# Fourier mixing: mirrored rows in another order, and the third piece of the second stage made once for two batches

## Chip, cores and metric

The kernel runs on one core of one Trainium2 chip. The metric is the device time of one execution in microseconds: 1210.03 us before, the median of three runs (1209.47 to 1211.12). The core has TensorE (PE, with its weight loads as PEld), VectorE (DVE), ScalarE (ACT), GpSimd (POOL) and SyncE (SP), which here only issues DMAs.

## The reference

Eight batches of eight heads, 576 positions, head size 64. Attention is causal by blocks of 64; its output x has 512 columns per position. Then comes a two-dimensional Fourier transform whose real part is added to x, a normalization, and a feed-forward layer (a feed, below).

```python
attn = softmax(where(mask, q @ k.T / 8, -1e9)); x = heads side by side of (attn @ v)   # 8 x 576 x 512
X = np.fft.fft(np.fft.fft(x, axis=1), axis=2)
u = x + np.real(X)
un = (u - mean(u)) / sqrt(var(u) + 1e-6)
out = u + np.maximum(un @ w_ch1, 0.0) @ w_ch2        # 512 -> 2048 -> 512
```

## The kernel before, in words

Every product is made in halves, a high and a low part of each operand, so that three products (high by high, high by low, low by high) stand for one. The inner loops all run on 128-row tiles; nearly every vector instruction is recorded under line 211 and every product under line 244, since two helpers issue them, so the names of tiles tell what they are.

**Attention.** Each of the 64 heads h gives five steps: a row maximum (`max_part`, `pair_max`), its transposition as a shift (`shift`, a DMA lead<-mt), the scores and their exponentials (`scores`: PSUM tile, ACT exp to p and cast to ph, POOL subtraction to pl), the value products (`values`, 45 products into av) and a division (DVE: DEN, rec, x). The x of two heads is written by DMA to a DRAM tile xd of the batch.

**Fourier, one batch b (`fourier_steps`, L862).** A real transform over 576 positions needs only the sums and differences of row s and its mirror 576 - s, so `mirror` (L865) loads rows in order (X, tiles LL) and mirrored rows by an indirect DMA (U, tiles UU), in three pieces c: 128 + 128 + 33 rows. `folded` (L886) makes the sums (name "c") and differences (name "s") of both rows and both column halves, and splits them into high and low part (tiles fs, un). `stage1` (L928) transforms over the positions, into z (zc0, zc1, zs0, zs1), with a middle column apart (`stage1_tail`, ZT). The second stage transforms over the columns: for each piece c, `stage2_sin` (L964) makes six products with z sine as weights, and `stage2_cos` (L980) seven with z cosine and ZT as weights and 258 columns moving; DVE makes difference and sum (dif, add) and POOL adds these to X and U in place (four additions). Piece 2 has 33 weight columns: row 288, which is its own mirror, and 32 pairs. It runs first, then pieces 0 and 1 (the loop at L1035). Row 288's result goes by DMA to row 0 of U piece 0 (L1006), whose mirror would be row 0 itself. The 32 + 32 results of piece 2 go by DMA to half of a tile `left`, which holds those of two batches.

**Feeds.** `normalized_steps` (L1052) normalizes two tiles, transposes them (ident,un) and queues a feed (`feed_steps`, L1112): 192 first products into ps or h (uh, ul), then gh on ACT and gl on DVE, then 96 second products into acc, an addition into u and the store. A batch has a feed for its low rows (X pieces 0 and 1) and one for its up rows (U pieces 0 and 1); four batches share one for the rests (two tiles `left`). That makes 18 feeds. In a batch with b % 4 == 3 the rests come first, then low, then up. Feeds 15 to 17 (`SEVEN`, L55) use a form with seven half products.

**What sets the order.** A planner (the loop at L1557) simulates all steps with assumed costs and emits instructions in its own order; each engine then runs its list strictly in that order. Steps stand in lanes (heads, maxima, scores, values, Fourier); the lanes' first steps compete by their `place`, and the products of the feed at the head of the queue are used as a filler wherever no other step is ready (L1592 to L1616). Feed 1 cannot begin before batch 0 is transformed, after head 7, and needs the weights W, which the side lanes prepare on DVE and ACT. `feed_number` (L1098) tells which feed a later step must wait for: the tiles of batch b - 2 must be free for `mirror`, and one step waits for the feed of the rests.

Of the kernel before, what the change touches and what calls it, by code (L numbers as in the profile page):

```python
# [91 lines left out]
def _constants():  # L92


    n = np.arange(NCOS)
    s = np.arange(LNH + 1)
# [4 lines left out]
    s_s[0] = 0.0  # L101
    s_s[LNH] = 0.0
    s_s[:, 0] = 0.0
    c_s[LNH, :LNH + 1] = (-1.0) ** n[:LNH + 1]
    k = np.arange(KCOL)
# [39 lines left out]
    p = np.arange(P)  # L145
    rows = np.stack([S - p, S - P - p, 320 - p % 32], 1)
    rows[0, 0] = rows[32, 2] = S
    return {
# [69 lines left out]
def tile_attn_fourier_ffn(  # L218
# [86 lines left out]
    for i in range(2):  # L305
        gpsimd.memset(MAIN[i], LEAST)
        gpsimd.memset(MAIN[i][0:64, 0:1], 0.0)
        gpsimd.memset(DIAG[i], LEAST)
    for i in range(HF):
        gpsimd.dma_start(LEAD[i][D:KS], c_masks)  # L310
        vector.tensor_scalar(LEAD[i][0:D, 0:64], ones[0:D, 0:64], 0.0, None, op0=ALU.mult)
    for i in range(2):
        vector.memset(VH[i][:, 0:4, :, D:D + 1], 1.0)
        vector.memset(VH[i][0:64, 4, :, D:D + 1], 0.0)
        vector.memset(VH[i][64:128, 4, :, D:D + 1], 1.0)
    for at in range(0, NCOS, P):
        w = min(P, NCOS - at)
        vector.tensor_scalar(ZT[:, at:at + w], ones[:, 0:w], 0.0, None, op0=ALU.mult)
# [543 lines left out]
    def fourier_steps(b):  # L862
        U, X, low, up, mine = [], [], [], [], []

        def mirror():  # L865
            xd = xs.pop(b)
            LL, UU = utile(), utile()
            U.extend((UU[:, 0], UU[:, 1], work.tile([97, DM], F32, name="U2", bufs=1)))
            X.extend((LL[:, 0], LL[:, 1], work.tile([33, DM], F32, name="X2", bufs=1)))
# [5 lines left out]
            U2 = U[2]  # L875
            sync.dma_start(X[2], xd[256:289])
            sync.dma_start(LL, xd[0:256].rearrange("(c p) d -> p c d", p=P))
            for dst, i in ((U2[0:33], 2), (U[0], 0), (U[1], 1)):
# [7 lines left out]
        def folded(op, width, name, c):  # L886
            r = (128, 128, 33)[c]
            e = work.tile([P, DM], F32, name="tmp", bufs=2)
            vector.tensor_tensor(e[0:r], X[c][0:r], U[c][0:r], op=op)
            vector.tensor_tensor(e[0:r, 1:256], e[0:r, 1:256], e[0:r, 511:256:-1], op=op)  # L890
            yield
# [8 lines left out]
            else:  # L900
# [3 lines left out]
                if name == "c":  # L904
                    rr = [U[2][64 + 32 * a:65 + 32 * a, 0:width].bitcast(F32R) for a in range(2)]
                    scalar.copy(rr[0], e[32:33, 0:width])
                yield
                vector.tensor_tensor(
                    t[32:64, 0:width], e[0:32, 0:width], t[0:32, 0:width].bitcast(F32), op=ALU.subtract
                )  # L910
# [17 lines left out]
        def stage1(name, m):  # L928
# [14 lines left out]
            vector.tensor_tensor(zz[:, 1], t[:, 0:n], zz[:, 0].bitcast(F32), op=ALU.subtract)  # L943
            yield

        def stage1_tail():
# [15 lines left out]
        bss = {}  # L962

        def stage2_sin(c):  # L964
            n = 128 if c < 2 else 32
            t = ps_tile()
            i = 0
            ns = slice(P * c, P * c + n)
            for m in range(2):
                for a, w in ((0, 0), (0, 1), (1, 0)):  # L970
                    mm(t[0:n, 0:KCOL], z["s", m][:, a, ns], sd[:, m, w], start=(i == 0), stop=(i == 5))
                    i += 1
            yield
            bs = bss[c] = work.tile([P, KCOL], F32, name="bs", bufs=1)
            if c == 2:
                gpsimd.memset(bs[32:33], 0.0)
            scalar.copy(bs[0:n], t[0:n, 0:KCOL])
            yield

        def stage2_cos(c):  # L980
            na, nb = (128, 128) if c < 2 else (33, 32)
            t = ps_tile()
            i = 0
            ns = slice(P * c, P * c + na)
            for m in range(2):
                for a, w in ((0, 0), (0, 1), (1, 0)):
                    mm(t[0:na, 0:KCOL], z["c", m][:, a, ns], cd[:, m, w], start=(i == 0), stop=False)
                    i += 1
            mm(t[0:na, 0:KCOL], ZT[:, ns], tail, start=False, stop=True)
            yield  # L990
# [6 lines left out]
            engine = gpsimd  # L997
            for u, lo, hi, n in ((X[c], dif, add, na), (U[c], add, dif, nb)):
                engine.tensor_tensor(u[0:n, 0:257], u[0:n, 0:257], lo[0:n, 0:257], op=ALU.add)
                engine.tensor_tensor(u[0:n, 257:512], u[0:n, 257:512], hi[0:n, 255:0:-1], op=ALU.add)  # L1000
            if c == 2:
                at = 64 * (b % 2)
# [19 lines left out]
        def stages(name):  # L1022
            for m in range(2):
                yield Step(
                    lambda m=m: stage1(name, m), 0.87, ("A0.42", "D0.47"), (D_("f" + name),),
                    D_("z" + name) if m == 1 else None, True, place=place,
                )
            if name == "c":
                yield Step(stage1_tail, 0.62, ("A0.4", "D0.46"), (D_("fc"),), D_("zt"), True, place=place)

        cos, sin = ("c", ALU.add, 257), ("s", ALU.subtract, 256)
        order = (folds(*cos), folds(*sin), stages("c"), stages("s"))
        for steps in order:
            yield from steps
        for c in (2, 0, 1):  # L1035
            yield Step(lambda: stage2_sin(c), 0.67, ("A0.38",), (D_("zs"),), D_("b", c), True, place=place)
            yield Step(
                lambda: stage2_cos(c), 0.78, ("D0.86", "B", "G3.0"), (D_("zc"), D_("zt"), D_("b", c)) + ((("F", feed_number(b - 1, 2)),) if c == 2 and b == 4 else ()), D_("u", c), True,
                place=place,
            )  # L1040
# [595 lines left out]
def _rows():  # L1636

    p = np.arange(P)
    up = S - p
    up[0] = LNH  # L1640
    return np.concatenate([p, P + p, up, S - P - p, 256 + p[0:32], 320 - p[0:32]])

# [23 lines left out]
```

## Time and profile before

| | |
|---|---|
| median of three runs | 1210.03 us (1209.47 to 1211.12) |
| the profiled execution, its own time | 1206.97 us |
| its span, first to last instruction | 1205.2 us |
| mean granted TensorE clock | 0.987 |
| TensorE's first product, end of its last | 8.03 us, 1201.1 us |
| feed 1 begins, heads 7 and 8 end | after 150 us; 95 and 154 us |
| products of the feed's halves | 3456 first, of 10338 in all recorded |

The profile has one row for a group of instructions: the engine, the operation, tile written <- tiles read, shapes and the count. In a timeline the first two columns are the start and the duration in us; a product's duration includes the way through the array, so products that follow each other overlap, and what one costs is read from start to start. "idle before <- X" is the time in which the engine had nothing to do, and what ended it. In the windows each engine's busy time has its count of instructions behind it.

### The profile page before, as it was taken

The page shows a single profiled execution, that of the slowest core. Times are in us where ns is not written, and L with a number is a line of the kernel's source. Part 1 is how long each engine was busy: PE and PEld are TensorE (multiplying, and loading weights), DVE is VectorE, ACT ScalarE, POOL GpSimd, SP SyncE. Part 2 cuts the span into 40 slices and gives each one's busy share as a digit, 9 for nine tenths or more (in the row PEclk, how much of TensorE's full clock was granted, in tenths as well). Part 3 has the DMA queues.
Part 4 walks back from the last instruction along what each step waited for, and adds up shares of the span by engine and source line. Part 5 has one row for each costly group of instructions (what it writes and reads, how often), then busy time and mean ns, then how long its engine had stood idle before and what let it go on. Part 6 is the DMA issues. An engine that isn't in the chain of part 4 may idle for free.

```text
span 1205.2 us, 26322 instructions
## 1 busy us (share of the span) xinstructions
PE 1136.7 (94%) x10338; PEld 839.3 (70%) x10338; DVE 746.8 (62%) x1615; ACT 622.4 (52%) x1338; POOL 487.8 (40%) x639
## 2 busy tenths in 40 slices
PE   5777797999999999999999999999999999999998
PEld 4554475676677777777777777777676767788885
DVE  6887888566867577675666758474657424534421
ACT  5666667755765566556565647654223212233320
POOL 4552625544652455345243355433333310535410
PEclk9998899999799999999999999999999999999999
DMA  8775454333452335242344033231010010000000
GB/s 261 234 231 176 144 132 105 89 111 102 112 136 72 93 84 159 72 119 76 105 116 137 28 100 114 85 95 41 28 41 18 23 58 1 23 10 10 18 18 18
DMA packets 66129, 108.28 MB, mean 90 GB/s; under 512 B 9671, under 2 KB 36209, under 8 KB 66006
## 3 DMA queue, kind: packets, MB, share of 16 engines
q1 hardware_dynamic: 58662, 82.25, 24.0%
q10 hardware_dynamic: 4384, 16.78, 4.2%
q0 software_dynamic: 2960, 7.58, 2.3%
q8 instruction: 81, 1.33, 0.5%
q14 instruction: 42, 0.34, 0.1%
HBM read 58.50 MB, written 18.89 MB: 64 GB/s over the span
## 4 chain that ended last, share of the span: by engine, by line
PE 81%; DVE 6%; DMA 4%; POOL 3%; ACT 3%; issue 2%; SPq 0%; ACTq 0%; DVEq 0%; POOLq 0%
PE acc L244 27%; PE ps L244 27%; PE h L244 18%; PE av L244 7%; DMA lead<-mt 2%; DVE W L211 2%; POOL pl L211 1%; POOL u L211 1%; DVE M L211 1%; PE ps L247 1%; DMA u<-in_moe_w_ch_dram 1%; ACT ph L211 1%; ACT left L211 1%; ACT p L211 1%; DMA lead<-lead 0%
## 5 line engine op out<-in xcount | busy, mean ns | idle before, releaser
L211 POOL TENSOR_TENSOR pl<-p,ph 128x288 f16<-128x288 f32 (+1 forms) x256 | 261.9, 1032 | 317.4 <-ACT ph L211 182.5
L244 PEld LDWEIGHTS <-W 128*128 128x128 f16 x3456 | 332.0, 98 | 59.1 <-issue 1.4
L244 PE MATMUL acc<-W,gh 128*128 128x512 f16 (+1 forms) x1008 | 288.7, 369 | 0.0
L244 PE MATMUL ps<-uh,W 128*128 128x256 f16 x1168 | 213.4, 273 | 0.6 <-issue 0.5
L244 PE MATMUL h<-uh,W 128*128 128x256 f16 x1136 | 211.9, 274 | 0.1
L244 PE MATMUL acc<-W,gl 128*128 128x512 f16 (+1 forms) x504 | 185.8, 369 | 0.0
L244 PE MATMUL ps<-ul,W 128*128 128x256 f16 x584 | 159.1, 272 | 0.0
L244 PE MATMUL h<-ul,W 128*128 128x256 f16 x568 | 155.6, 274 | 0.0
L244 PEld LDWEIGHTS <-ph 128*128 128x128 f16 x2112 | 133.0, 103 | 30.6 <-issue 5.2
L244 PEld LDWEIGHTS <-gh 128*128 128x128 f16 x1056 | 98.2, 98 | 70.9 <-issue 3.9
L244 PE MATMUL ps<-lead 72*128 72x192 f16 (+11 forms) x510 | 115.5, 292 | 19.4 <-DMA lead<-in_c_masks_dram 8.0
L211 DVE TENSOR_REDUCE M<-ps 128x2 fp32r<-128x128 f32 (+4 forms) x214 | 93.2, 469 | 56.7 <-PE ps L244 54.4
L244 PE MATMUL av<-VH,pl 128*128 128x65 f16 (+1 forms) x963 | 116.9, 201 | 10.6 <-POOL pl L211 7.4
L244 PE MATMUL av<-VH,ph 128*128 128x65 f16 (+1 forms) x966 | 118.1, 203 | 1.1 <-ACT p L211 0.7
L244 PE MATMUL av<-VL,ph 128*128 128x64 f16 x960 | 116.5, 200 | 0.0
L244 PEld LDWEIGHTS <-pl 128*128 128x128 f16 x1056 | 103.1, 102 | 14.6 <-POOL pl L211 10.0
L211 DVE SCALAR_TENSOR_TENSOR gl<-ps,gh 128x512 f16<-128x512 f32 x73 | 50.2, 687 | 91.8 <-ACT gh L211 91.3
L211 ACT ACTIVATE gh<-ps 128x512 f16<-128x512 f32 x73 | 43.3, 594 | 119.3 <-PE ps L244 115.4
L211 ACT ACTIVATE p<-ps 128x288 f32<-128x288 f32 (+1 forms) x164 | 81.7, 499 | 41.8 <-PE ps L244 35.2
L211 ACT CAST ph<-p 128x512 f16<-128x512 f32 (+1 forms) x188 | 98.2, 523 | 5.1
L244 PEld LDWEIGHTS <-lead 73*128 73x128 f16 (+1 forms) x744 | 66.3, 104 | 38.6 <-issue 14.0
L244 PEld LDWEIGHTS <-gl 128*128 128x128 f16 x528 | 51.4, 97 | 55.1 <-DVE gl L211 0.4
(280 smaller groups left out, 1993.6 us busy)
## 6 DMA issues: line engine op xcount, KB each, us to landing
raw<-in_qk_dram SPq DMA_DIRECT2D x30, 576.0 KB
W<-in_moe_w_ch_dram ACTq DMA_DIRECT2D x14, 1024.0 KB
V<-in_v_dram SPq DMA_DIRECT2D x32, 320.0 KB
rest<-lead SPq DMA_DIRECT2D x64, 144.0 KB
rest<-rest SPq DMA_DIRECT2D x60, 144.0 KB
out_dram<-u SPq DMA_DIRECT2D x32, 256.0 KB
xd<-x SPq DMA_DIRECT2D x30, 256.0 KB
lead<-lead SPq DMA_DIRECT2D x60, 72.0 KB
```

Of the source, the lines that this page charges most:

```text
L211: x = f(*args, **kw)
L244: return tc.keep_in_program_order(nc.tensor.matmul(*args, **kw))
L247: return tc.keep_in_program_order(nc.tensor.transpose(*args, **kw))
```

## The change

The rows are put in another order. Positions 1 to 256 become pieces 0 and 1; piece 2 is now row 0, rows 257 to 287 and row 288. So both self-mirrored rows, 0 and 288, stand in piece 2, and pieces 0 and 1 need nothing of it: the DMA to row 0 of U goes, the low and up feeds wait for pieces 0 and 1 only, and the 33 + 31 results of piece 2 serve the rests alone. The constants are permuted in the same way.

The third piece of the second stage is made once for two batches. Each `stage1` copies its last 33 (32) columns of z, high and low, into a shared tile ZP at column 0 (even b) or 64 (odd b), on ACT; `stage1_tail` does so into ZTP. The odd batch then runs one pass with 97 columns of weights. X2 and U2 become two fixed tiles of 128 rows, with the even batch at row 0 and the odd at row 64; they and the ZP tiles are zeroed at the start. In an odd batch the pass stands between the low and the up rows' normalization, and the rests of four batches now come last, after the up rows.

```diff
+    X2, U2 = (const.tile([P, DM], F32, name=x) for x in ("X2", "U2"))
+    gpsimd.memset(X2, 0.0)
+    gpsimd.memset(U2, 0.0)
+    ZP = {(name, m): const.tile([P, 2, width], F32R, name=f"zp{name}{m}") for name, width in (("c", 98), ("s", 96)) for m in range(2)}
+    ZTP = const.tile([P, 98], F32R, name="ztp")
     for i in range(HF):
         gpsimd.dma_start(LEAD[i][D:KS], c_masks)
...
-            sync.dma_start(X[2], xd[256:289])
-            sync.dma_start(LL, xd[0:256].rearrange("(c p) d -> p c d", p=P))
+            sync.dma_start(X[2][0:1], xd[0:1])
+            sync.dma_start(X[2][1:33], xd[257:289])
+            sync.dma_start(LL, xd[1:257].rearrange("(c p) d -> p c d", p=P))
...
+            w = 33 if name == "c" else 32
+            scalar.copy(ZP[name, m][:, :, o:o + w], zz[:, :, 256:256 + w].bitcast(F32))
+            yield
...
+            scalar.copy(ZTP[:, o:o + 33], ZT[:, 256:289].bitcast(F32))
+            yield
...
-            na, nb = (128, 128) if c < 2 else (33, 32)
+            na, nb = (128, 128) if c < 2 else (97, 96)
...
-                sync.dma_start(mine[0][at:at + 32], X[2][0:32])
-                sync.dma_start(mine[0][at + 32:at + 64], U[2][0:32])
-            elif c == 0:
-                sync.dma_start(U[0][0:1], X[2][32:33])
+                for at in (0, 64):
+                    sync.dma_start(mine[0][at:at + 33], X2[at:at + 33])
+                    sync.dma_start(mine[0][at + 33:at + 64], U2[at + 1:at + 32])
...
-        for c in (2, 0, 1):
+        def second_stage(c):
...
+        for c in range(2):
+            yield from second_stage(c)
         uu = tuple(D_("u", c) for c in range(3))
+        yield from normalized_steps(low, uu[0:2], (store(b, 0), store(b, 1)), place)
+        if b % 2:
+            yield from second_stage(2)
+        yield from normalized_steps(up, uu[0:2], (store(b, 2), store(b, 3)), place)
         if b % 4 == 3:
             us = list(lefts)
             lefts.clear()
             yield from normalized_steps(us, uu[2:], (rest_store(b - 3), rest_store(b - 1)), place)
-        yield from normalized_steps(low, uu[0:2], (store(b, 0), store(b, 1)), place)
-        yield from normalized_steps(up, uu, (store(b, 2), store(b, 3)), place)
...
-        return 2 * b + 1 + b // 4 if i == 2 else 2 * b + 1 + (b + 1) // 4 + i
+        return 2 * b + 1 + b // 4 + i
```

The planner makes a new order of the whole program from this. At the start of the program, GpSimd's list before (MAIN and DIAG are small tiles of the maxima, lead the tiles of the first two heads, which get the masks):

```order
L211 MEMSET MAIN_102 64x1
L211 MEMSET DIAG_104 128x5
L211 DMA lead_93<-in_c_masks_dram 9x1216
L211 DMA lead_94<-in_c_masks_dram 9x1216
L211 ISA
L211 TENSOR_TENSOR rest_95<-raw,lead_93 64x576
```

and after (X and U are the new fixed tiles X2 and U2):

```order
L211 MEMSET MAIN_102 64x1
L211 MEMSET DIAG_104 128x5
L211 MEMSET X_118 128x512
L211 MEMSET U_119 128x512
L211 DMA lead_93<-in_c_masks_dram 9x1216
L211 DMA lead_94<-in_c_masks_dram 9x1216
L211 ISA
L211 TENSOR_TENSOR rest_95<-raw,lead_93 64x576
```

Two zeroings of 128 x 512 have come ahead of the masks' DMAs.

On ScalarE, in the transform of batch 1, the list before, from its first sine part zs to the first copy bs of the second stage (gh belongs to feed 2, p and ph to the scores, lead and rest to the split of a pair of heads):

```order
L211 CAST zs_3899<-ps_3856 128x288
L211 ACTIVATE gh<-h_3747 128x512
L211 CAST zs_3911<-ps_3882 128x288
L211 ACTIVATE p_3917<-ps_3894 128x512
L211 CAST ph_3892<-p_3917 128x512
L211 ACTIVATE lead_528,vacc<-raw 128x576
L211 ACTIVATE rest_529,vacc<-raw 128x576
L211 ACTIVATE p_3972<-ps_3921 128x512
L211 CAST ph_3919<-p_3972 128x512
L211 COPY bs<-ps_3950 32x258
```

and after, in the same place, from the last cosine copies on:

```order
L211 CAST ZT<-ps_4187 2x290
L211 CAST un<-tmp 128x256
L211 CAST zpc_122<-zc_4219 128x2x33
L211 CAST zpc_123<-zc_4230 128x2x33
L211 ACTIVATE mt<-ps_4217 5x128
L211 CAST ztp<-ZT 128x33
L211 ACTIVATE tmp,vacc<-V 128x640
L211 CAST zs_4281<-h_4253 128x288
L211 CAST zs_4285<-h_4270 128x288
L211 CAST zps_124<-zs_4281 128x2x32
L211 CAST zps_125<-zs_4285 128x2x32
L211 COPY bs<-h_4308 128x258
```

Five copies into zpc, ztp and zps have come in; feed 2's gh, which stood between the two zs, now stands earlier, and no feed's instruction is left in this place. The list before has 31 instructions from feed 2's last gh to feed 3's first uh, the list after has 82; on VectorE there are 47 and 102 between feed 2's last gl and feed 3's first ul. Along TensorE's list no product of a feed stands for two to three heads there before and for five after, and head 18's last value product is the last before the stretch in both.

More of the change, by code (lines that the diff above doesn't have):

```diff
@@ L92, in _constants @@
 def _constants():
-    n = np.arange(NCOS)
-    s = np.arange(LNH + 1)
+    n = np.concatenate([np.arange(1, 257), [0], np.arange(257, NCOS)])
+    s = n[:LNH + 1]
     ang = 2.0 * np.pi / S
@@ L100, in _constants @@
     s_s = np.sin(ang * ((s[:, None] * n[None, :NSIN]) % S))
-    s_s[0] = 0.0
+    s_s[256] = 0.0
     s_s[LNH] = 0.0
-    s_s[:, 0] = 0.0
-    c_s[LNH, :LNH + 1] = (-1.0) ** n[:LNH + 1]
+    s_s[:, 256] = 0.0
+    c_s[LNH, :LNH + 1] = (-1.0) ** s
     k = np.arange(KCOL)
@@ L145, in _constants @@
     p = np.arange(P)
-    rows = np.stack([S - p, S - P - p, 320 - p % 32], 1)
-    rows[0, 0] = rows[32, 2] = S
+    rows = np.stack([S - 1 - p, S - 1 - P - p, 320 - p % 32], 1)
+    rows[0, 2] = rows[32, 2] = S
     return {
@@ L315, in tile_attn_fourier_ffn @@
         vector.memset(VH[i][64:128, 4, :, D:D + 1], 1.0)
+    vector.tensor_scalar(ZTP, ones[:, 0:98], 0.0, None, op0=ALU.mult)
+    for t in ZP.values():
+        for x in range(2):
+            vector.tensor_scalar(t[:, x], ones[:, 0:t.shape[2]], 0.0, None, op0=ALU.mult)
     for at in range(0, NCOS, P):
@@ L867, in mirror @@
             LL, UU = utile(), utile()
-            U.extend((UU[:, 0], UU[:, 1], work.tile([97, DM], F32, name="U2", bufs=1)))
-            X.extend((LL[:, 0], LL[:, 1], work.tile([33, DM], F32, name="X2", bufs=1)))
+            U.extend((UU[:, 0], UU[:, 1], U2[o:o + 33]))
+            X.extend((LL[:, 0], LL[:, 1], X2[o:o + 33]))
             low.extend(X[0:2])
@@ L874, in mirror @@
             mine.append(lefts[-1])
-            U2 = U[2]
-            sync.dma_start(X[2], xd[256:289])
-            sync.dma_start(LL, xd[0:256].rearrange("(c p) d -> p c d", p=P))
-            for dst, i in ((U2[0:33], 2), (U[0], 0), (U[1], 1)):
+            sync.dma_start(X[2][0:1], xd[0:1])
+            sync.dma_start(X[2][1:33], xd[257:289])
+            sync.dma_start(LL, xd[1:257].rearrange("(c p) d -> p c d", p=P))
+            for dst, i in ((U[2], 2), (U[0], 0), (U[1], 1)):
                 gpsimd.indirect_dma_start(
@@ L904, in folded @@
                 if name == "c":
-                    rr = [U[2][64 + 32 * a:65 + 32 * a, 0:width].bitcast(F32R) for a in range(2)]
+                    spare = work.tile([P, KCOL], F32, name="add", bufs=1)
+                    rr = [spare[x:x + 1, 0:width].bitcast(F32R) for x in (o + 32, 64)]
                     scalar.copy(rr[0], e[32:33, 0:width])
@@ L960, in stage1_tail, with last @@
             yield
+            scalar.copy(ZTP[:, o:o + 33], ZT[:, 256:289].bitcast(F32))
+            yield
         bss = {}
+        def last(name, m, a):
+            return ZP[name, m][:, a, 0:97 if name == "c" else 96]
         def stage2_sin(c):
-            n = 128 if c < 2 else 32
+            n = 128 if c < 2 else 96
             t = ps_tile()
@@ L970, in stage2_sin @@
                 for a, w in ((0, 0), (0, 1), (1, 0)):
-                    mm(t[0:n, 0:KCOL], z["s", m][:, a, ns], sd[:, m, w], start=(i == 0), stop=(i == 5))
+                    lhs = z["s", m][:, a, ns] if c < 2 else last("s", m, a)
+                    mm(t[0:n, 0:KCOL], lhs, sd[:, m, w], start=(i == 0), stop=(i == 5))
                     i += 1
@@ L975, in stage2_sin @@
             if c == 2:
-                gpsimd.memset(bs[32:33], 0.0)
+                gpsimd.memset(bs[96:97], 0.0)
             scalar.copy(bs[0:n], t[0:n, 0:KCOL])
@@ L986, in stage2_cos @@
                 for a, w in ((0, 0), (0, 1), (1, 0)):
-                    mm(t[0:na, 0:KCOL], z["c", m][:, a, ns], cd[:, m, w], start=(i == 0), stop=False)
+                    lhs = z["c", m][:, a, ns] if c < 2 else last("c", m, a)
+                    mm(t[0:na, 0:KCOL], lhs, cd[:, m, w], start=(i == 0), stop=False)
                     i += 1
-            mm(t[0:na, 0:KCOL], ZT[:, ns], tail, start=False, stop=True)
+            mm(t[0:na, 0:KCOL], ZT[:, ns] if c < 2 else ZTP[:, 0:97], tail, start=False, stop=True)
             yield
@@ L997, in stage2_cos @@
             engine = gpsimd
-            for u, lo, hi, n in ((X[c], dif, add, na), (U[c], add, dif, nb)):
+            for u, lo, hi, n in ((X[c] if c < 2 else X2, dif, add, na), (U[c] if c < 2 else U2, add, dif, nb)):
                 engine.tensor_tensor(u[0:n, 0:257], u[0:n, 0:257], lo[0:n, 0:257], op=ALU.add)
```

20 lines of the change are left out of this document (10 added, 10 removed).

## Prediction

> **What bounds the kernel now.** I read the page first: busy shares, then the chain that ended last.
>
> ```profile
> PE 1136.7 (94%) x10338; PEld 839.3 (70%) x10338; DVE 746.8 (62%) x1615; ACT 622.4 (52%) x1338; POOL 487.8 (40%) x639
> PE 81%; DVE 6%; DMA 4%; POOL 3%; ACT 3%; issue 2%; SPq 0%; ACTq 0%; DVEq 0%; POOLq 0%
> ```
>
> TensorE is busy for 94% and makes 81% of the chain, so the question is where the other 68.5 us are. The windows answer it (columns: PE, PEld, DVE, ACT, POOL, granted clock, DMA share, GB/s).
>
> ```profile
> 0.00:30.00 30.00, 15.89 (x93) 13.58 (x94) 20.01 (x55) 17.71 (x37) 13.22 (x25) 1.00 0.88 262
> 30.00:90.00 60.00, 44.00 (x398) 31.04 (x397) 50.66 (x108) 37.55 (x88) 31.66 (x35) 1.00 0.77 232
> 120.00:150.00 30.00, 21.37 (x143) 13.41 (x142) 24.14 (x33) 20.50 (x43) 18.51 (x24) 0.90 0.46 142
> 284.80:317.40 32.60, 27.09 (x257) 19.48 (x257) 23.46 (x60) 20.16 (x46) 21.85 (x27) 0.79 0.45 127
> 300.00:310.00 10.00, 7.01 (x52) 4.21 (x52) 8.17 (x19) 7.03 (x18) 8.97 (x12) 0.56 0.28 81
> 360.00:1200.00 840.00, 836.96 (x7634) 627.25 (x7632) 476.06 (x1026) 385.37 (x816) 314.48 (x434) 1.00 0.22 63
> ```
>
> From 360 us on TensorE is idle for 3 of 840 us, at full clock: there a product that goes is time that goes. Before, there are stalls: while heads run with no feed to fill in (0 to 150 us), and once more from 285 to 317 us, between feed 2 and feed 3. In that stretch VectorE is busy 72% (23.46 of 32.6), against 84% in the early one (50.66 of 60), and no engine is full.
>
> **The change, part by part.** First the third piece. The timeline of TensorE for the last batch shows a pass with 33 columns of weights and one with 128.
>
> ```profile
> 1022.83 0.96 PE L244 MATMUL h<-dft,zc 128*33 128x258 f32 x6
> 1023.62 0.28 PE L244 MATMUL h<-dft,ZT 128*33 128x258 f32 x1
> 1023.75 0.87 PE L244 MATMUL h<-dft,zs 128*128 128x258 f32 x6
> 1024.45 0.28 PE L244 MATMUL ps<-uh,W 128*128 128x256 f16 x1
> ...
> 1025.69 0.96 PE L244 MATMUL ps<-dft,zc 128*128 128x258 f32 x6
> 1026.49 0.28 PE L244 MATMUL ps<-dft,ZT 128*128 128x258 f32 x1
> 1026.61 0.88 PE L244 MATMUL ps<-dft,zs 128*128 128x258 f32 x6
> 1027.33 0.60 PE L244 MATMUL acc<-W,gh 128*128 128x512 f16 x2
> ```
>
> From start to start, six products take 0.70 to 0.72 us (1023.75 to 1024.45, 1026.61 to 1027.33), 0.119 each. A pass of 6 + 7 products is 13 x 0.119 = 1.55 us; four passes of eight go: 4 x 1.55 = **-6.2 us**. Three of them (batches 2, 4, 6) lie where TensorE is full; the first lies in the stalled stretch at 125 us, so the bounds are -4.7 and -6.2, and I take the whole, since what it gives up is needed by feed 1 right behind.
>
> The pair's pass loads 97 columns of weights where the single one loaded 33. In the rows, the seven products with 33 columns take 0.92 us (1022.83 to 1023.75) and the seven with 128 also 0.92 (1025.69 to 1026.61). So a wider load costs nothing. The Trainium skill (TensorE: Matmul & The Clock Gate, "LDWEIGHTS (loading the stationary operand)") speaks against this part: the load's time grows with the columns, about P / 1.2 ns. By that alone, as an estimate from the page, 97 columns instead of 33 would be 53 ns dearer for each of 52 products, 2.8 us in all; the trace does not show it, because loads run beside products.
>
> On the other engines the four passes take along four copies on ACT, eight subtractions and additions on DVE and sixteen additions on POOL. What comes in is 40 small copies on ACT (five a batch), which wait for DVE's low parts of z.
>
> ```profile
> L211 ACT CAST zc<-ps 128x290 fp32r<-128x290 f32 x12 | 4.8, 401 | 13.8 <-PE ps L244 13.8
> L211 ACT ACTIVATION_READ_ACCUMULATOR tmp<-V 128x1 f32 x32 | 6.1, 189 | 0.0
> ```
>
> The trace has no copy of 33 to 66 columns from SBUF; 290 columns take 0.40 us and a single one 0.19. I take 0.25, so 1.25 us a batch. Behind the last of the five stands the copy of bs, which waits for TensorE's sine products (0.7 us) anyway; the cover is that and ACT's idle half, so **0**; without cover it would be 1.25 us for each batch, mostly in the stretch of batch 1, which is in the term below. Bounds 0 and +1.25. The DMAs balance: mirror adds one issue a batch on SP (xd to X2 in two pieces) and one goes (X2 to U row 0); those to the rests stay sixteen. GpSimd's gathers stay three a batch.
>
> **The start.** The zeroing of the two new 128x512 tiles stands on GpSimd ahead of the masks' DMAs.
>
> ```profile
> 2.54 1.06 POOL L211 DMA_DIRECT2D lead<-in_c_masks_dram  x2
> 8.03 1.62 PE L244 MATMUL ps<-lead 72*128 72x64 f32 x5 [8.03 <-DMA lead<-in_c_masks_dram]
> 1003.58 0.31 POOL L211 MEMSET bs<- 1x258 f32 x1
> ```
>
> TensorE's first product waits for that DMA until 8.03. A memset of 258 columns takes 0.31 us, so 512 columns at most 0.62, two of them 1.2. Bounds 0 (if the landing is set by the traffic, DMA share 0.88 there, and not by the issue) and +1.2. I take half, **+0.6**, since VectorE has 10 of its 30 us idle there and catches some up. The nine small zeroings on VectorE lie ahead of its first wait.
>
> **The end.** The last feed is now the rests, whose store is two DMAs for each tile instead of one.
>
> ```profile
> 1201.30 0.99 SPq L211 DMA_DIRECT2D out_dram<-u  x2
> ```
>
> An issue takes 0.5 us, the last one comes two issues later: +1.0, less something for the half-sized piece; **+0.8**, bounds 0 and +1.0.
>
> **Batch 0.** The chain of waits runs through GpSimd's third piece before the other two:
>
> ```profile
> 127.67 0.72 POOL X L211
> 128.39 1.39 POOL U L211 x2
> ```
>
> With that piece gone, pieces 0 and 1, and so feed 1, can start up to 2.8 us (0.72 x 4) earlier; but what is late next is VectorE, busy 24.14 of 30 us with weights there. Half: **-1.3**, bounds -2.8 and 0.
>
> **Batch 1, the term that decides.** The new order has one stretch without any feed's products, as before, but a longer one. Counted along TensorE's order from feed 2's last first-half product to feed 3's first, with start-to-start spacings, it is 21.7 us of products before and 35.8 now; VectorE has 47 instructions between feed 2's last gl and feed 3's first ul before, 102 now; ACT 31 and 82. Two to three heads stood there, now five: batch 1's folds are spread over more heads, while feed 2 is eaten up at head 18 in both.
>
> ```profile
> 284.15 0.69 DVE L211 SCALAR_TENSOR_TENSOR gl<-h,gh 128x512 f16<-128x512 f32 x1
> ...
> 313.88 0.68 DVE L211 TENSOR_TENSOR ul<-ps,uh 128x512 f16<-128x512 f32 x1
> 317.45 0.27 PE L244 MATMUL ps<-uh,W 128*128 128x256 f16 x1
> ```
>
> Before: 284.8 to 317.4 is 32.6 us for 21.7 of products, a stall of 10.9. Now: of the 102 VectorE instructions 38 are short ones of about 0.18 us; in the window 21 of 60 are, so a long one is (23.46 - 21 x 0.18) / 39 = 0.505, and 102 are 38 x 0.18 + 64 x 0.505 = 39.2 us. ACT's 82 at 20.16 / 46 = 0.44 are 36 us. At the early stretch's share, 84%, 39.2 becomes 46.4 us, with the same 3.5 from ul to the first product 49.9, a stall of 14.1: **+3.2**. If VectorE never idled it would be 42.7, a stall of 6.9 (-4.0); at the 72% of the present stretch 57.9, a stall of 22.1 (+11.2). I take 84% because that stretch is heads without feeds, as this one is, where the present one is mostly one batch's chain of waits on GpSimd.
>
> Sum: -6.2 + 0 + 0.6 + 0.8 - 1.3 + 3.2 = **-2.9 us**. The profiled execution took 1206.97 (span 1205.2 and 1.8 around it), 3.1 below the median of 1210.03; I carry the difference over to the median: **1207.1**.
>
> **The rivals.** *The stretch eats the saving* (ends slower): VectorE and ACT work through batch 1's longer stretch no better than through the present one, 72%. For it: three engines have 36 to 39 us there, in program order, each waiting for the others. Against: five heads give more to overlap than two. Price: -2.9 - 3.2 + 11.2 = +5.1, **1215.1**. It decides once the stretch, now 32.6, goes past 52.8 us (46.4 + 3.5 + 2.9).
>
> *The stretch costs nothing more*: five heads fill it so well that its stall stays about 10.9. Then -2.9 - 3.2 = -6.1, **1203.9**.
>
> *The clock falls.* From 300 to 310 us the granted clock was 0.56 with TensorE busy 7 of 10 us; if it stays there through the longer stretch, 35.8 us of products become 35.8 / 0.56 = 64, a stall of 28, 17 more than before: -2.9 - 3.2 + 17 = +11, **1221**. Against it stands the window 30 to 90: 44 of 60 us busy, and the clock is 1.00. The Trainium skill states that rule (TensorE: Matmul & The Clock Gate, "HAM oscillation — how this bites in real kernels"): no idle gap over about 3.4 us between bursts of products, or the clock falls to half; the trace agrees that it falls near a stall, and the window 30 to 90 that a partly idle TensorE keeps it.
>
> *Later order*: all later instructions are interleaved anew, and small stalls (3 us after 360) may come or go; then the gain is lost in them, about 1209.5. That the change does not do what it says is excluded: the order has 52 products fewer.
>
> **How the numbers follow.** A measurement of this kernel can tell 0.2%, 2.4 us, from no change. The forecast gets 0.45; its own range is -6 to 0 around -2.9, of which 0.26 lies below -2.4 and 0.19 within. The full saving gets 0.20 (faster), the longer stretch 0.25 (slower), the clock 0.04 (slower), the later order 0.06 (same). So faster 0.46, same 0.25, slower 0.29. The range: the low end takes the full saving with the lower bounds of batch 0 and the stretch, about -9: 1201. The high end takes the longer stretch and a start and end at their bounds, +6: 1216. Outside are the clock and the far ends.
>
> **What would show it.** Right: 52 products fewer; the stretch of batch 1 at 47 to 53 us with VectorE at 80 to 88%; TensorE's first product at 8.5 to 9.2 us; products of the pair's pass still 0.119 apart; TensorE full from there on. Wrong: a stretch past 53 us, or a clock under 0.8 through it; ACT's copies of the columns ending waits of TensorE; new stalls after 360 us of more than 5 us together.

## The result, and the profile after

The changed kernel takes 1237.6 us (median of 4 runs, 1236.5 to 1241.7) against 1209.75 (1209.1 to 1211.1): ratio 1.0238, 95% interval 1.0217 to 1.0259. It is slower by 28 us; 1207.1 was forecast, and the range ended at 1216. The profiled execution took 1241.7, of which the span is 1239.9. Medians leave out single executions that took over 20% longer than the rest of their kernel.

The page of the profile after: busy time, share and instructions of each engine, and the chain that ended last (the work that follows back from the last instruction, by engine).

```profile
PE 1142.2 (92%) x10286; PEld 839.3 (68%) x10286; DVE 734.8 (59%) x1616; ACT 630.3 (51%) x1374; POOL 466.6 (38%) x621
PE 67%; DMA 2%; DVE 2%; ACT 1%; POOL 1%; issue 0%; SPq 0%; another core or an unknown queue 0%; DVEq 0%; ACTq 0%; POOLq 0%
```

The 52 products are gone (10338 to 10286), POOL has 621 instructions instead of 639, and ACT 36 more, its 40 copies less four. The work is what the diff says. Yet TensorE is idle for 97.7 us instead of 68.5. Where, the windows tell (columns: PE, PEld, DVE, ACT, POOL, granted clock, DMA share, GB/s); of before first:

```profile
30.00:150.00 120.00, 88.81 (x639) 57.52 (x638) 97.27 (x183) 78.96 (x171) 57.81 (x71) 0.95 0.63 196
250.00:400.00 150.00, 143.77 (x1440) 105.14 (x1439) 105.38 (x245) 93.98 (x210) 66.08 (x77) 0.95 0.37 103
400.00:840.00 440.00, 436.97 (x4459) 322.05 (x4458) 288.59 (x674) 260.74 (x575) 190.40 (x227) 1.00 0.34 94
```

and of the changed kernel:

```profile
30.00:150.00 120.00, 85.83 (x632) 56.43 (x631) 95.81 (x186) 77.06 (x172) 53.07 (x67) 0.89 0.62 193
250.00:400.00 150.00, 134.41 (x1357) 97.64 (x1356) 103.36 (x241) 97.58 (x219) 71.83 (x83) 0.93 0.41 113
400.00:840.00 440.00, 426.39 (x4366) 312.85 (x4365) 275.89 (x657) 261.33 (x581) 179.18 (x212) 0.99 0.35 95
840.00:1190.00 350.00, 347.86 (x2676) 267.72 (x2675) 160.94 (x298) 101.33 (x205) 108.37 (x192) 1.00 0.06 21
286.05:341.31 55.26, 42.52 (x443) 31.36 (x442) 41.85 (x105) 39.44 (x91) 29.32 (x34) 0.85 0.45 125
```

From 250 to 400 us TensorE is idle for 15.6 us instead of 6.2, from 400 to 840 for 13.6 instead of 3.0. The first is batch 1's stretch: the last row runs from feed 2's last gl to feed 3's first product, 55.3 us with VectorE busy 76%. The second is where before TensorE was full, and where the prediction expected nothing. Of the 29 us that TensorE is idle longer these two stretches make 20; the other 9 lie at the start (2.9 us up to 30 us), from 30 to 150 us (3.0) and behind 840 us (2.1, and 1.5 behind the last product). The waits of TensorE behind 400 us (waiter, releaser, us in all, times, longest) name the largest:

```profile
PE h L244 <- DMA lead<-mt: 5.8, 1, 5.8
PE av L244 <- ACT ph L211: 1.8, 1, 1.8
PE ps L244 <- DMA lead<-mt: 1.8, 1, 1.8
```

"lead<-mt" is the shift of a head, 5 rows of 256 bytes that SP copies to the last row of lead. Rows of the timeline around that wait (start, duration, engine, instruction):

```profile
565.33 0.25 ACT L211 ACTIVATE mt<-h 5x128 f16<-5x128 f32 x1
...
566.36 0.83 SPq L211 DMA_DIRECT2D left<-X  x1
...
567.73 0.66 SPq L211 DMA_DIRECT2D left<-U  x1
...
568.44 0.81 SPq L211 DMA_DIRECT2D left<-X  x1
...
569.35 0.63 SPq L211 DMA_DIRECT2D left<-U  x1
...
570.07 0.76 SPq L211 DMA_DIRECT2D lead<-mt  x1
...
576.28 0.40 PE L244 MATMUL h<-lead 73*128 73x288 f16 x1 [5.75 <-DMA lead<-mt]
```

The shift was ready at 565.6. SP first waited for GpSimd's sums and issued the four copies into the pair's rest tile (X in 33 rows, U in 31, twice); the shift's copy went out at 570.8 and was usable only at 576.3. Right behind its issue the DMA engines were nearly empty; from 572 us on the next head's copies, issued behind the shift, fill them:

```profile
571.00:572.00 1.00, 0.00 (x0) 0.00 (x0) 0.00 (x0) 0.00 (x0) 0.83 (x3) 1.00 0.08 24
```

A share of 0.08 of 16 engines is 1.3 engines, and 24 GB/s is one row of 2 KB every 0.085 us. The packets of the trace show these rows one behind the other, from 569.0 to 575.2; four of the shift's five rows went at 571.5, the fifth at 575.3, behind the last of them. So it looks as if one DMA engine carried the 31 rows of left<-U, twice, 62 x 0.085 = 5.3 us, and the shift's fifth row waited for that engine. The same seems to happen at 356 us, where TensorE waits 2.9 us for a shift behind four such copies.

At the start, rows of the timeline:

```profile
2.65 0.53 POOL L211 MEMSET X<- 128x512 f32 x1
...
3.12 0.52 POOL L211 MEMSET U<- 128x512 f32 x1
...
3.59 1.06 POOL L211 DMA_DIRECT2D lead<-in_c_masks_dram  x2
...
10.42 0.39 PE L244 MATMUL ps<-lead 72*128 72x64 f32 x1 [10.42 <-DMA lead<-in_c_masks_dram]
```

The two memsets move the masks' DMAs by 1.05 us, and the first product by 2.4.

### The profile page after: what moved, and what is told of

Same layout as the page of the kernel before. It is cut to its first block, busy times and chain, and to the rows that moved or that the text cites. A ratio compares the mean times of both kernels' runs of the same rounds, so it can differ in the third digit from the quotient of the medians.

```text
span 1239.9 us, 26215 instructions
## 1 busy us (share of the span) xinstructions
PE 1142.2 (92%) x10286; PEld 839.3 (68%) x10286; DVE 734.8 (59%) x1616; ACT 630.3 (51%) x1374; POOL 466.6 (38%) x621
## 3 DMA queue, kind: packets, MB, share of 16 engines
q1 hardware_dynamic: 58294, 82.23, 23.7%
## 4 chain that ended last, share of the span: by engine, by line
PE 67%; DMA 2%; DVE 2%; ACT 1%; POOL 1%; issue 0%; SPq 0%; another core or an unknown queue 0%; DVEq 0%; ACTq 0%; POOLq 0%
PE acc L244 23%; PE ps L244 22%; PE h L244 15%; PE av L244 5%; DMA lead<-mt 1%; PE ps L247 1%; DMA rest<-lead 0%; SPq L211 0%; PE h L247 0%; ACT p L211 0%; ACT ph L211 0%; POOL ag L211 0%; POOL pl L211 0%; DVE M L211 0%
## 5 line engine op out<-in xcount | busy, mean ns | idle before, releaser
L211 POOL TENSOR_TENSOR pl<-p,ph 128x288 f16<-128x288 f32 (+1 forms) x256 | 258.0, 1016 | 363.2 <-ACT ph L211 184.4
L244 PE MATMUL ps<-uh,W 128*128 128x256 f16 x1264 | 231.4, 273 | 0.2 <-DVE M L211 0.2
L244 PE MATMUL h<-uh,W 128*128 128x256 f16 x1040 | 198.5, 277 | 1.1 <-DVE M L211 0.5
L244 PE MATMUL ps<-ul,W 128*128 128x256 f16 x632 | 172.4, 273 | 0.0
L244 PE MATMUL h<-ul,W 128*128 128x256 f16 x520 | 143.9, 277 | 0.1
L211 DVE TENSOR_REDUCE M<-ps 128x1 fp32r<-128x192 f32 (+4 forms) x209 | 93.2, 484 | 71.7 <-PE ps L244 71.6
L244 PE MATMUL ps<-lead 72*128 72x64 f16 (+11 forms) x495 | 115.3, 296 | 16.2 <-DMA lead<-in_c_masks_dram 10.4
L211 DVE SCALAR_TENSOR_TENSOR gl<-ps,gh 128x512 f16<-128x512 f32 x79 | 54.3, 688 | 103.8 <-ACT gh L211 103.3
L211 ACT ACTIVATE p<-ps 128x512 f32<-128x512 f32 (+1 forms) x162 | 81.3, 502 | 48.6 <-PE ps L244 40.7
L211 ACT ACTIVATE gh<-ps 128x512 f16<-128x512 f32 x79 | 46.9, 593 | 111.8 <-PE ps L244 106.4
```

What stands on the lines that cost most here:

```text
L211: x = f(*args, **kw)
L244: return tc.keep_in_program_order(nc.tensor.matmul(*args, **kw))
```

## The experiments

Two theories stood after this. **Own costs**: the change's additions are slow at places that can be named and mended (the rests' copies, the memsets). **Order**: the planner puts the same instructions in another order, and the order of before was a lucky or a chosen one. Times below are medians; each ratio is against the kernel before on the same chip, and its 95% interval stands behind it. The kernel before had a median of 1208.3 to 1210.1 us on the four chips that were used, so a difference between two medians below can be off by 1 to 2 us.

### The rests' copies, 32 rows each

```
-rows[0, 2] = rows[32, 2] = S
+rows[0, 2], rows[32, 2] = 0, S
...
-sync.dma_start(X[2][0:1], xd[0:1])
+sync.dma_start(X[2][0:1], xd[S:S + 1])
...
-sync.dma_start(mine[0][at:at + 33], X2[at:at + 33])
-sync.dma_start(mine[0][at + 33:at + 64], U2[at + 1:at + 32])
+sync.dma_start(mine[0][at:at + 32], X2[at + 1:at + 33])
+sync.dma_start(mine[0][at + 32:at + 64], U2[at:at + 32])
...
```

The list by which the rows of the output are put back is permuted to match.

> The changed kernel, with row 0 of the sequence kept in U2 instead of X2, so that the four copies into a pair's rest tile have 32 rows each instead of 33, 31, 33 and 31. Every other instruction stands where it stood. Theory 'one DMA engine': the 31 rows of 2 KB run one after the other, and the shift's copy to lead that SP issues next waits behind them; then TensorE's waits of 5.9 us at 570 us and of 3.0 us at 356 us fall to under 1 us together and the time falls from 1237.6 by 7 to 9 us, to 1229 to 1231. Rival 'late sums': the shift's copy is late because SP waited for GpSimd's sums before it could issue the rests' copies; then the waits stay above 4 us together and the time falls by less than 3 us.

Measured: 1229.6 us (four runs, 1224.4 to 1232.2), ratio 1.0152 (1.0112 to 1.0193), 8 us less than the changed kernel, as the first theory said. The timeline at the same place:

```profile
561.96 0.56 SPq L211 DMA_DIRECT2D left<-X  x1
563.33 0.53 SPq L211 DMA_DIRECT2D left<-U  x1
563.91 0.59 SPq L211 DMA_DIRECT2D left<-X  x1
564.59 0.54 SPq L211 DMA_DIRECT2D left<-U  x1
565.22 0.74 SPq L211 DMA_DIRECT2D lead<-mt  x1
...
567.02 0.28 PE L244 MATMUL h<-lead 73*128 73x288 f16 x1 [0.89 <-DMA lead<-mt]
```

SP still waits for the sums, and TensorE's wait falls from 5.75 to 0.89 us: the copies of 31 rows were the cause, the late sums were not. The wait at 356 us is gone. The two falls, 4.9 and 2.9 us, add up to about the 8. The Trainium skill states the rule (DMA: Bandwidth & Descriptors, "Why a DMA increments its semaphore by 16 and not by 1"): a DMA issued by SP runs on the largest number of engines up to 16 that divides the rows, and on the lowest-numbered ones. By it 31 rows run on one engine, 33 on eleven, 32 on sixteen, and the shift's 5 rows on five, one of which is the busy one. The trace agrees for the 31 rows (one behind the other) and for the five (four at once, one late).

### The memsets behind the masks' DMAs

```
-gpsimd.memset(X2, 0.0)
-gpsimd.memset(U2, 0.0)
 for i in range(HF):
     gpsimd.dma_start(LEAD[i][D:KS], c_masks)
...
+gpsimd.memset(X2, 0.0)
+gpsimd.memset(U2, 0.0)
 vector.tensor_scalar(ZTP, ones[:, 0:98], 0.0, None, op0=ALU.mult)
```

> The changed kernel, with the zeroing of X2 and U2 on GpSimd behind the two DMAs of the masks instead of ahead of them; the order of all other instructions is the same. If the two memsets alone hold up the start, TensorE's first product goes from 10.4 us back to about 8.0 and the time falls by about 2.4 us, to 1235. Rival: the start comes back, but VectorE and GpSimd bound the stalled first 150 us, so less than 1 us of it reaches the end.

Measured: 1232.4 us, ratio 1.0192 (1.0162 to 1.0221), 5.2 us less. The timeline of TensorE:

```profile
7.95 0.61 PE L244 MATMUL ps<-lead 72*128 72x64 f32 x2 [7.95 <-DMA lead<-in_c_masks_dram]
```

The start comes back to 7.95 us, and nothing of it is lost on the way, against the rival. Why the gain is 5.2 and not 2.4 is not shown; the spread of medians covers 1 to 2 us of it.

### Both mends

> The changed kernel with both mends, the rests' copies of 32 rows and the memsets behind the masks' DMAs; everything else stands where it stood. If the two prices are apart from each other they add up: 1237.6 - 8.0 - 5.2 = 1224.4, within 2 us. If the late stalls move when the start moves (one price twice), 1228 or more. What is left above before would be the order's and the stretch's, some 15 us.

Measured: 1218.6 us, ratio 1.0081 (1.0063 to 1.0098): 19.0 us less than the changed kernel, more than the 13.2 of the two apart. Neither forecast came, the sum (1224.4) or one price twice (1228 or more); why the two together are worth more is not shown. Windows:

```profile
250.00:400.00 150.00, 137.50 (x1448) 100.18 (x1445) 102.08 (x249) 100.94 (x228) 75.06 (x86) 0.95 0.44 121
400.00:840.00 440.00, 434.31 (x4408) 319.40 (x4405) 284.78 (x672) 263.43 (x586) 178.82 (x210) 1.00 0.34 92
```

TensorE's idle time from 400 to 840 us falls from 13.6 to 5.7 us, from 250 to 400 us, where batch 1's stretch lies, from 15.6 to 12.5. These two prices are about two thirds of the loss. What is left is 10 us above before, where the passes alone should have brought it 6 below.

### Before, in another order

The planner's table of costs gets the entries that the change gives it, and the kernel does the same work:

```
...
-0.87, ("A0.42", "D0.47"), (D_("f" + name),)
+0.87, ("A0.42", "D0.47", "A0.25"), (D_("f" + name),)
...
-("A0.4", "D0.46"), (D_("fc"),)
+("A0.4", "D0.46", "A0.23"), (D_("fc"),)
...
```

> The kernel before, with nothing added to its work: only the planner's table of costs for the first stage gets the entries of 0.25 and 0.23 us of ScalarE that the change adds to it, so the same instructions come in another order. Theory 'own costs' (the loss of the changed kernel comes from what it adds): within 0.2% of before, 1207 to 1212. Rival 'another order' (the planner's order of before happens to be good, and any edit of its table loses several us): 1214 or more, with new waits of TensorE behind 270 us.

Measured: 1217.3 us, ratio 1.0064 (1.0042 to 1.0086). 8 us are lost by an edit that changes no work, as the rival said. Batch 1's stretch is as short as before; from 400 to 840 us TensorE is idle for 8.4 us instead of 3.0, which is most of the loss. The longest of its waits there (waiter, releaser, us in all, times, longest):

```profile
PE h L244 <- DVE add L211: 6.2, 2, 3.1
```

and the rows around one of the two:

```profile
422.54 0.72 POOL L211 TENSOR_TENSOR u<-u,dif 128x255 f32<-128x255 f32 x1
423.30 0.43 DVE L211 TENSOR_TENSOR dif<-h,bs 128x258 f32<-128x258 f32 x1 [4.95 <-POOL u L211]
423.64 0.42 DVE L211 TENSOR_TENSOR add<-h,bs 128x258 f32<-128x258 f32 x1
424.11 0.27 PE L244 MATMUL h<-uh,W 128*128 128x256 f16 x1 [3.09 <-DVE add L211]
```

VectorE's dif for one piece has a single buffer (`bufs=1`), which GpSimd's sums of the piece before still read; so the PSUM tile h stays full and a feed's products, planned into it, wait. The step that makes dif has no entry for that buffer in the planner's table. A third order, by MARGIN 0.28 instead of 0.3 (how long, in the planner's simulation, another step must have been ready to be taken ahead of a feed's product that is ready):

> The kernel before with the planner's MARGIN 0.28 instead of 0.3: the same instructions in a third order. Theory 'order': several us off before in either direction, with other late waits; the kernel before has an order that suits it, so rather slower: 1212 to 1220. Rival 'own costs': within 2.4 us of before.

Measured: 1217.0 us, ratio 1.0059 (1.0037 to 1.0082), as forecast. Two edits without any work in them cost 7 to 8 us each: the order of before is the best of the three.

### Before, with four passes fewer, planned anew and in place

The second stage's third piece is left out in batches 0, 2, 4 and 6, once so that the planner does not know the steps (`for c in (2, 0, 1) if b % 2 else (0, 1)`):

> The kernel before, without the third piece's second stage in the four even batches (their part of the output is left unfinished), and nothing else of the change. The planner orders anew. Theory 'own costs': the 52 products that go are worth what they last, 6.2 us: 1203 to 1205. Rival 'another order': the saving is lost or more than lost in waits that the new order brings, 1208 or more.

and once so that it plans them and they issue nothing (below, "in place"; the same in `stage2_cos`). The two copies into left stay in both, so part of the output is left unfinished:

```
 def stage2_sin(c):
+    if c == 2 and b % 2 == 0:
+        yield
+        yield
+        return
...
```

> The kernel before in its own order, word for word, without the instructions of the third piece's second stage in the four even batches (52 products, 4 copies, 8 VectorE and 16 GpSimd instructions and 4 memsets; that part of the output is left unfinished). The planner still plans them, so nothing else moves. If the prediction's first term is right, 6.2 us less: 1203.5, at least 4.7 less. Rival: what goes at one place is given back at waits behind it, under 3 us less.

Measured: planned anew 1219.3 us, ratio 1.0083 (1.0055 to 1.0110); in place 1201.2, ratio 0.9938 (0.9922 to 0.9955). The same work left out is worth 7 us in the old order (4.7 were forecast at least), and costs 10 in a new one. Windows of the second:

```profile
250.00:400.00 150.00, 143.41 (x1460) 105.00 (x1458) 107.00 (x248) 95.67 (x214) 65.47 (x76) 0.97 0.37 104
400.00:840.00 440.00, 437.90 (x4464) 322.59 (x4463) 286.25 (x671) 261.17 (x574) 189.41 (x224) 1.00 0.33 94
```

Idle time is that of before; only the products are fewer.

### The changed work in other orders

Both mends, and MARGIN 0.25 or 0.1:

> The kernel with both mends, and only the planner's MARGIN 0.25 instead of 0.3, so the same instructions stand in another order. Theory 'order': what is left of the loss belongs to this one order and not to the change, so another order of the same work differs by more than 6 us, and this one may come below 1216. Rival 'stretch': batch 1's longer stretch without a feed is a property of the change, so it stays near 28 us of stall and the time within 3 us of the run with both mends.

> The kernel with both mends and MARGIN 0.1: a third order of the changed work beside 1218.6 (MARGIN 0.3) and 1215.4 (0.25). Theory 'order': another time again, between 1205 and 1225. If the loss belonged to the change's work and not to its order, all three would lie within 3 us.

Measured: 1215.4 (ratio 1.0051, 1.0036 to 1.0066) and 1222.0 (1.0108, 1.0087 to 1.0129). The expectation of more than 6 us between 0.3 and 0.25 failed (3.2), but the three do not lie within 3 us. And the length of batch 1's stretch is no property of the change: between the first-half products of feeds 2 and 3 lie 57.6 us with MARGIN 0.3, 42.6 with 0.25 and 35.4 with 0.1 (34.2 in before, 59.5 in the changed kernel). Windows with 0.1:

```profile
250.00:400.00 150.00, 142.18 (x1435) 105.88 (x1434) 105.50 (x245) 94.78 (x218) 68.85 (x80) 0.97 0.39 106
400.00:840.00 440.00, 432.18 (x4405) 315.47 (x4403) 286.97 (x666) 267.09 (x594) 186.96 (x215) 0.99 0.35 95
```

The idle time from 250 to 400 us is down to 7.8 us; from 400 to 840 us it is 7.8 now, where it was 5.7. So none of the three orders is as good as that of before.

### ScalarE's small copies

In the changed order with both mends, and in the order of before (next section), without the 40 copies, so that the pair's tiles stay zero:

> The kernel with both mends without ScalarE's 40 small copies into the pair's tiles, which stay zero (the rests come out wrong for that); the planner still plans them, so the order of all the rest is the same. Prediction's term of 0: within 1.5 us of the run with both mends. Rival: the copies lengthen batch 1's stretch and the folds' chains, 3 us or more less.

> The pair in the order of before with the mends, without ScalarE's 40 small copies (the pair's tiles stay zero and the rests come out wrong for it). Prediction's term of 0: within 1.5 us of 1208.25. Rival: they are what the pair costs of its own, 3 us or more below.

Measured: 1220.1, ratio 1.0091 (1.0074 to 1.0108), against 1.0081 with them; and 1206.8, ratio 0.9974 (0.9960 to 0.9989), against 0.9996 (0.9983 to 1.0009). Not the 3 us of the rival; between nothing and 2.7 us, and the intervals of the two last ratios overlap.

### The pair in the order of before

The planner is given the steps of before; in the even batches the third piece's steps issue nothing, and a small copy is issued with VectorE's subtraction ahead of it. This also takes back the two places that the change gives by intent: the pass between the two normalizations, and the rests last.

```
-for c in range(2):
+for c in (2, 0, 1):
     yield from second_stage(c)
 uu = tuple(D_("u", c) for c in range(3))
+if b % 4 == 3:
+    us = list(lefts)
+    lefts.clear()
+    yield from normalized_steps(us, uu[2:], (rest_store(b - 3), rest_store(b - 1)), place)
 yield from normalized_steps(low, uu[0:2], (store(b, 0), store(b, 1)), place)
-if b % 2:
-    yield from second_stage(2)
-yield from normalized_steps(up, uu[0:2], (store(b, 2), store(b, 3)), place)
+yield from normalized_steps(up, uu, (store(b, 2), store(b, 3)), place)
...
 def stage2_cos(c):
...
+    if c == 2 and b % 2 == 0:
+        yield
+        yield
+        yield
+        return
...
```

> The changed kernel with both mends, brought into the order of before word for word: the planner is given the steps of before (third piece first, an unused one in the even batches too, the rests' feed ahead of low and up, no entries for the small copies), and the unused steps issue nothing. So all of the change's work is there and nothing is re-ordered. Theory 'order': the loss was the order's and the mends', so what is left is the saving of the passes: 1201 to 1204, faster than both kernels. Rival: the pair's pass, the copies or the sums of 97 rows cost something of their own; then 1208 or more.

> The same in the order of before, but with the memsets ahead of the masks' DMAs and the rests' copies of 33 and 31 rows, as the change has them. If the two have prices of their own, it is 8 to 13 us above the run with the mends. Rival: in this order the shift's copies do not stand right behind the rests' copies, and the start's 2.4 us are partly caught up; then 0 to 4 us above it.

Measured: 1208.25, ratio 0.9996 (0.9983 to 1.0009), and without the mends 1220.2, ratio 1.0094 (1.0073 to 1.0116). So the order was 10 us, the mends 12 here. But 7 us were to be gained, and none was: the forecast of 1201 to 1204 failed. Rows of the timeline at the first fold of batch 0:

```profile
107.48 0.51 SPq L211 DMA_DIRECT2D lead<-lead  x1
...
108.03 0.59 SPq L211 DMA_DIRECT2D lead<-rest  x1
...
108.67 0.60 SPq L211 DMA_DIRECT2D rest<-rest  x1
...
109.31 0.59 SPq L211 DMA_DIRECT2D rest<-lead  x1
...
109.95 0.59 SPq L211 DMA_DIRECT2D raw<-in_qk_dram  x1
...
110.58 1.11 POOL L211 DMA_DIRECT2D fs<-add  x2 [5.36 <-ACT add L211]
...
116.90 0.58 PE L244 MATMUL h<-dft,fs 98*128 98x290 f32 x1 [2.83 <-DMA fs<-add]
```

The same place in before, SP's instructions:

```profile
105.39 0.76 SPq L211 DMA_DIRECT2D lead<-mt  x1
128.41 0.60 SPq L211 DMA_DIRECT2D left<-X  x1
```

In before SP stood still from 106 to 128 us: its copies into left and to row 0 of U waited for GpSimd's sums, and the next head's copies waited behind them. The change takes these waits away in batch 0. So five transfers start at 107 us, 1.0 MB by their sizes (72, 72, 144, 144 and 576 KB); the two single rows for the folds, issued at 110.6 us, land at 116.4 in the trace, 5.8 us later, where in before it was 3.3. The window from 112 to 116 us shows what they meet (next to last column: DMA share), here

```profile
112.00:116.00 4.00, 2.07 (x7) 1.48 (x6) 2.72 (x6) 1.51 (x3) 0.00 (x0) 0.50 1.02 378
```

and in before, with the two microseconds ahead of it:

```profile
110.00:111.00 1.00, 0.35 (x2) 0.29 (x1) 0.96 (x3) 0.60 (x1) 0.89 (x4) 0.51 1.04 430
111.00:112.00 1.00, 1.00 (x5) 0.86 (x3) 0.53 (x3) 0.86 (x3) 0.09 (x1) 0.50 0.80 310
112.00:116.00 4.00, 4.00 (x13) 3.09 (x13) 3.74 (x9) 2.56 (x7) 0.00 (x0) 0.50 0.01 2
```

In before, too, the rows were issued into traffic, but it ended at 112 us and they landed at 112.6. Here it lasts until 116, and so do they. The changed kernel has the same wait, 3.7 us.

### A copy that waits, put back

A copy of one row on SP that waits for GpSimd's sums of piece 0 and that nobody reads, at the place where before had its copy to row 0 of U:

```
+elif c == 0:
+    gate = dram.tile([1, DM], F32, name="gate")
+    sync.dma_start(gate, U[0][0:1])
```

For batch 0 alone the condition is `c == 0 and b == 0`. (The transfers that it holds back are 1.0 MB, not the 0.6 of the first expectation.)

> The pair in the order of before with the mends, and in every batch a copy of 2 KB on SP (row 0 of the finished piece 0 to a scratch row in DRAM, read by nobody) at the place where before copied row 0 of the sequence from X2 to U. It waits for GpSimd's sums as that copy did, and SP's copies of the next head wait behind it. Theory 'vanished wait': that copy held 0.6 MB of head copies and loads back in batch 0; without it they fill the DMA engines at 112 to 116 us, and the two single rows for the folds land 5.8 us after issue instead of 3.3, so TensorE waits 2.8 us. With the copy back this wait falls under 0.5 us, the time by 2.5 to 4, to 1204 to 1206. Rival: the rows are late because of their new source rows; then the wait and the time stay.

> The same with the copy in batch 0 alone. If only batch 0's wait matters, as with the copy in all batches, 1204 to 1206; if the later ones hold back SP where it is needed, 1 to 2 us below that run; if they too keep transfers apart, above it.

> The changed kernel in its own order with both mends and the copy that waits, in all batches. Theory 'vanished wait': its wait of 2.8 us for the same rows at 113 us goes too, so 1218.6 becomes 1214 to 1216. Rival: in this order the copy blocks SP where the next heads' copies are needed, and the time stays or grows.

Measured: 1205.05 (ratio 0.9963, 0.9940 to 0.9986) in all batches, 1205.9 (0.9962, 0.9946 to 0.9977) in batch 0 alone, and in the changed order 1223.7 (1.0114, 1.0088 to 1.0140). TensorE's waits from 90 to 150 us with the copy in batch 0 alone have this row:

```profile
PE h L244 <- DMA fs<-add: 0.9, 1, 0.9
```

The wait falls from 2.8 to 0.9 us (in all batches it is gone), and the pair is faster than both kernels by its interval, 0.4% below before. That is 4 us less than without the copy, of which the wait explains 1.9 to 2.8. In the changed order the wait goes as well, to 0.8, and yet the time does not fall, as the rival said. There TensorE's idle time from 400 to 840 us grows from 5.7 to 8.9 us, of which its waits for lead<-mt are only 1.1 (2.5 to 3.6), so what takes the gain is not settled.

## Why the prediction was wrong

Two of the prediction's own signs of being wrong came: a stretch past 53 us, and more than 5 us of new stalls behind 360 us. Term by term:

**The passes, -6.2**: right. In place 7 us.

**The wider load, 0, and the copies, 0 (bounds 0 and +1.25 a batch)**: right in kind. In the changed kernel, from 345 us on, products with 96 and 97 columns of weights stand 0.119 to 0.123 us apart (medians), those with 32 and 33 in before 0.119 to 0.120, so the wider load cost nothing that can be seen. A copy of 64 or 66 columns took 0.24 us where 0.25 was estimated; leaving all out changed the time by +1.2 us in one order and -2.7 in the other, by the ratios.

**"The DMAs balance"**: the step that failed first; it was put at nothing. The DMAs were counted, and their shape and their waits were not. Copies of 31 rows go through one DMA engine, 5.3 us for two, with the next head's shift behind them: 8 us. And the copies that the change takes away in batch 0, into left and to row 0 of U, had held back SP: without them 1.0 MB of copies and loads fall on the folds' single rows, for which TensorE waits 2.8 us.

**The start, +0.6 (bounds 0 and +1.2)**: undersized beyond its bound. The memsets took 0.53 and 0.52 us, less than the 0.62 that was estimated, but 1.05 us later at the issue became 2.4 at TensorE's first product: the zs loads, issued by SP at 3.0 and 3.6 us, now stand ahead of the masks' DMAs, where the first of these was ahead of both (2.54 us); that this is why is argued, not tried apart. The prediction took the traffic only as what could hide a later issue. Putting the memsets later gave back 5.2.

**The end, +0.8**: last product to end of span is 5.6 us against 4.1, +1.5. The four stores' issues took 2.46 us, 0.6 each and not 0.5.

**Batch 0, -1.3**: nothing came. With both mends, so with the start of before, feed 1's first product stands at 150.2 us, in before at 150.0. With the waiting copy put back it stands at 147.5: the wait for the folds' rows had taken the place of GpSimd's third piece (single profiled executions).

**Batch 1's stretch, +3.2**: 55.3 us where 49.9 was forecast, VectorE at 76% and not 84%. That is past the 52.8 us from which the first rival decides, and nearer to its 72%. The prediction also set two stretches against each other that are not the same: products counted from feed 2's last first-half product, time taken from its last gl, which comes 1.6 us later in before and 4.2 us later now. Between the first-half products themselves, of before and of the changed kernel, the windows are:

```profile
283.24:317.45 34.21, 28.70 (x267) 20.46 (x265) 24.61 (x61) 21.09 (x48) 22.59 (x29) 0.80 0.46 130
281.80:341.31 59.51, 46.77 (x491) 34.02 (x489) 46.06 (x114) 41.67 (x97) 29.32 (x34) 0.86 0.42 116
```

With the 21.7 and 35.8 us of products that were counted, that is a stall of 12.5 before and 23.7 now, 11.2 more, as much as the rival put in: its mechanism was right for this order. But 11.2 instead of 3.2 makes the sum +5.1 us, and the miss is 30; and three orders of the same work show that the length of the stretch belongs to this order (57.6, 42.6 and 35.4 us between the feeds).

**Later order, about 1209.5, chance 0.06**: the other step that failed, by its size. It was held to small stalls because before had 3 us of them. But before is the best order of those tried: two others of the very same work lie 7 to 8 us above it. That from 360 us on "a product that goes is time that goes" was seen in this order alone. With the same work and the same mends the changed order takes 1218.6 us and the old one 1208.25: 10 us are the order's, the stretch and the end's 1.5 us among them, and what is due to the change's two places by intent is not told apart from the planner's reordering. So the account is -7 for the passes, +4 for the vanished wait, +3 open, +10 for the order and +19 for what the two mends give back, +29, where +28 was measured. It is a chain of differences between runs, and so must come out near the whole; what it shows is the parts.

**The clock**, the rival at 1221: no. Over the stretch its mean was 0.86, in before 0.80, not 0.56. In the two windows above TensorE's idle time grew by 7.2 us (5.5 to 12.7); slower products can make at most the other 4 of the 11.2.

What stays open: between the 7 us of the passes left out and the 4 us that the pair with the waiting copy gains lie 3 us. The 40 copies may be part of them, and so may longer waits for the shifts (behind 265 us TensorE waits 1.0 us for lead<-mt with the passes left out, 1.8 with the pair and the copy in batch 0); no run tells it apart from the spread. Open is also why the two mends together are worth 19 us and apart 13.

## What to carry to other kernels

Where a planner sets the order, price an edit in the old order first, by steps that are planned and issue nothing: that separates what the work is worth from what a new order costs. Of a DMA that comes, goes or changes shape, read its rows (31 rows go through one engine) and its waits (what stood behind it on its queue, and what that now collides with), not its count. A delay ahead of the first transfers can land as twice as much (1.05 us became 2.4 here).

## What was not expected of the hardware

- 33 rows of 2 KB took 0.80 to 0.85 us to issue, 31 rows 0.62 to 0.68, 32 rows 0.51 to 0.60. While copies of 31 rows ran alone, 24 GB/s were moved, and a transfer of five short rows behind two of them was usable 5.4 us after the end of its issue, where it took 1.1 us behind copies of 32 rows.
- Single rows of 1 KB issued by GpSimd landed 3.3 us after their issue where other traffic (a share of 0.80 to 1.04) ended 2.7 us after it, and 5.8 us after it where a share of 1.02 went on.
